# First pair's attention operands formed in place by 64-column transposes, under a new order of the work

## The chip, the cores and the metric

The kernel runs on one core of a Trainium2 chip. The metric is the device time of one execution in microseconds; below, us is microseconds and ns nanoseconds. TensorE multiplies matrices and transposes (PE, with its weight loads as PEld), VectorE is DVE, ScalarE is ACT, GpSimd is POOL, and SP issues the DMA transfers. Each engine takes its instructions strictly in the order in which they were issued to it.

## The reference

Three layers follow each other: an attention in which a query sees only keys of its own cluster (2 batches, 8 heads, 768 tokens, 64 wide, 16 centroids a head), a feed-forward layer with a soft gate and a layer norm, and a second one that multiplies two projections. All is float32.

```python
q_assign = argmax(einsum('bhsd,hcd->bhsc', q_n, c_n), -1)
k_assign = argmax(einsum('bhsd,hcd->bhsc', k_n, c_n), -1)
scores = scale * q @ k.T, where q_assign == k_assign, else -1e9
x = softmax(scores) @ v                      # to 1536 x 512
h = x @ w_in;  s = h * softmax(h)            # 512 -> 1024
x = (layernorm(s) * g_ln) @ w_out            # -> 512
out = ((x @ w_a) * (x @ w_b)) @ w_out2       # 512 -> 1536 -> 512
```

## The kernel before

Every float32 operand of a product is held as a pair hi + lo of 12-bit parts, and three of the four products are taken. Tokens sit on partitions in tiles of 128, six tiles to a head. Heads are worked in eight pairs, n = 0 to 7. One tile's step is: `score` (L727: four matmuls into a PSUM bank, the DVE maximum L731, the ACT exponential L735), `turn` (L759: six transposes, with ACT L776 and DVE L251 splitting the result into hi and lo) and, after every second tile, `apply` (L791: twelve matmuls with v, then merges L806, L811, L812 on ACT and POOL).

A head's score needs an operand block of four slots, `kqv(h)`, 128 rows by 768 tokens. Rows 0 to 63 and 64 to 127 of a slot hold different parts: q hi and q lo together, k hi twice, q hi again beside the query one-hots, k lo beside the key one-hots. Before the change that block is filled for every head in the same way. `qk_part` (L478) turns two tokens of a head at once with 128-column transposes, so that the result holds even tokens on partitions 0 to 63 and odd tokens on 64 to 127; ACT writes hi and DVE (for q, L495) or POOL (for k of the first pair, L486 and L488) writes lo into a side buffer, `hlv`. `do_place` then moves the parts to their rows: six DMAs a head (L512), save that for head 0 two of the six are ACT copies (L510, `PLACE`). For the first pair `do_sim` (L534, L535) multiplies the side buffer with the normalized centroids `cb`, DVE sums the parts (L538), `do_arg` (L591 to L602) finds the one-hot of the best centroid, and `do_oh0` (L617) turns the one-hots, which ACT (L628) and DVE (L626) write to rows 64 to 79 of two slots.

Weights arrive as the bits of float64. `weight` (L326 to L359) loads 512 of them a partition and makes float32 hi and lo: ACT or POOL scales the top word (L328, L330), DVE shifts and joins (L335, L343, L346), POOL joins the low word (L340, L350), ACT makes hi (L359) and DVE or POOL lo (L249, L251). Eight such loads make `w_in` for the first feed-forward layer, whose first matmul (L914) starts at 279 us; the four early ones are issued in the first 30 us.

The order of all this is made by a planner, `Plan`. Each work item is added with an engine, an estimated length, a rank and the buffer cells that it reads and writes. Dependencies follow the order in which the items are added; `schedule` then runs a list schedule in which each engine, when it becomes free, takes the item of lowest rank that is ready within 60 ns by the estimates, and the instructions are issued in the order found. So an estimate that is off puts an item into an engine's queue where it will wait on the chip. For a transfer the estimate is that SP is held for its cost and that it lands 1850 ns later, however many are under way:

```python
def dma(cost, rank, fn, reads, writes):
    pl.add("SP", max(cost, 650), rank, fn, reads, writes, after=1850 + min(0, cost - 650))
```

A 512 KB weight load has cost 1456 (ns); a place transfer has 275, 820 or 546 for 96, 288 or 192 KB. At the start 39 transposes of the identity (L451, `FILL`) have the lowest priority and fill TensorE's waiting time.

Of the kernel before, what the change touches and what calls it, by code (L numbers as in the profile page):

```python
# [8 lines left out]
F32 = mybir.dt.float32  # L9
# [23 lines left out]
P1 = {'a': -6.508, 's': 0.229, 'do_place': 16.159, 'do_v': -8.279, 'do_sims': 3.084, 'do_arg': -13.543, 'do_oh': -1.51, 'do_ohd': -29.092, 'qk_part': -21.079}  # L33
BR = {'h': 3.102, 'ln': 2.949, 'lnt': 7.533, 'x2': 11.917, 'dm': 0.03, 'ts': 2.583}


class Plan:
    """Work items in program order, each with its engine, an estimate of its
    length, a rank and the cells of the buffers it reads and writes. emit() issues
    them in the order of a list schedule that keeps every dependency."""  # L40
# [6 lines left out]

    def __init__(self):
        self.ops = []
        self.last = {}  # L50

    def add(self, eng, cost, rank, fn, reads=(), writes=(), after=0.0):
# [34 lines left out]
    def schedule(self):  # L87
# [9 lines left out]
        ready = {}  # L97
# [3 lines left out]
        for i in range(n):  # L101
            if not left[i]:
                ready.setdefault(ops[i][0], []).append(i)
        order = []
        while len(order) < n:
# [11 lines left out]
            end = self.pe_end(cols, s, ops[i][1]) if eng == "PE" else s + ops[i][1]  # L117
            free[eng] = end
            order.append((s, i))
            for j in succ[i]:  # L120
# [7 lines left out]
                if not left[j]:  # L128
                    ready.setdefault(ops[j][0], []).append(j)
# [8 lines left out]
def cells(buf, *spans, rows=3):  # L138
    """Cells of 128 floats of a buffer, for each half of the partitions."""
# [7 lines left out]
def dve(n):  # L147
    return n / 0.96 + 69
# [6 lines left out]
def act(n, sbuf=False):  # L155
    return n / 1.2 + (93 if sbuf else 51)

# [6 lines left out]
def tile_cluster_attention_moe_moe2(  # L164
# [1012 lines left out]
```

## Time and profile before

| | us |
|---|---|
| median of 3 runs | 747.77 |
| lowest and highest run | 745.48, 748.54 |
| span of the profiled execution | 746.8 |
| TensorE busy in it | 717.1 (96%) |
| DVE, ACT, POOL busy | 468.8, 397.9, 341.3 |
| bytes moved by DMA | 60.74 MB |

The profile of one execution lies within the three runs, 1.0 us below their median. A busy share alone says little here: it counts the fillers, and instructions that run at half clock count for twice their time. So the table is to be read by stretches, each with its idle time and its granted clock: 0 to 17.8 us until the first score, then attention with everything else beside it until 290 us, the first feed-forward layer until 450 us, and the second one, which starts at 419.5 us beside the first, to the end.

### The profile page before, as it was taken

What the parts mean: (1) busy time and instruction counts of PE and PEld (TensorE: products, weight loads), DVE (VectorE), ACT (ScalarE), POOL (GpSimd) and SP (SyncE); (2) the same over time, 40 slices, a digit from 0 to 9 for tenths busy, and PEclk for the clock granted to TensorE, in tenths of its full rate; (3) what the DMA queues carried; (4) which work ended last, traced back from release to release, by engine and by line L of the source; (5) the groups of instructions that cost most, each with busy time, mean ns of one, the idle gap of its engine ahead of it and who ended that gap; (6) DMA issues with size and microseconds to landing.
All of it is one profiled execution on the core that took longest, in us unless ns stands there. A gap on an engine that the chain in (4) does not pass through costs nothing.

```text
span 746.8 us, 12308 instructions
## 1 busy us (share of the span) xinstructions
PE 717.1 (96%) x4441; PEld 661.7 (89%) x4441; DVE 468.8 (63%) x866; ACT 397.9 (53%) x870; POOL 341.3 (46%) x429
## 2 busy tenths in 40 slices
PE   7888999999999999899899999999999999999997
PEld 7787898899999988689899999989999999999996
DVE  5995899988888887999975657631136311122222
ACT  3686898999998996565433634432133312111111
POOL 6657988958658326465513777820027300000000
PEclk7898999999999999999999999999999999999999
DMA  8774665453435001222300433320003000101011
GB/s 218 185 173 130 154 159 154 112 156 97 127 75 124 17 1 56 85 86 86 114 29 29 127 127 115 113 85 1 1 1 113 29 1 1 42 1 43 1 42 43
DMA packets 40573, 60.74 MB, mean 81 GB/s; under 512 B 3896, under 2 KB 35392, under 8 KB 40512
## 3 DMA queue, kind: packets, MB, share of 16 engines
q1 hardware_dynamic: 40512, 59.95, 28.7%
q8 instruction: 35, 0.57, 0.3%
q14 instruction: 26, 0.21, 0.1%
HBM read 36.74 MB, written 3.15 MB: 53 GB/s over the span
## 4 chain that ended last, share of the span: by engine, by line
PE 64%; DVE 16%; ACT 6%; issue 4%; POOL 4%; DMA 4%; SPq 0%; DVEq 0%; ACTq 0%; POOLq 0%
PE psS L1090 12%; PE psT L1062 11%; PE psO L791 7%; PE psS L727 6%; PE psT L759 6%; PE psM L1062 6%; PE psO L1062 6%; PE psS L914 3%; DVE F L346 3%; DVE R L251 2%; PE psO L1003 2%; POOL F L350 2%; DVE F L335 2%; PE psM L1003 2%; DMA F<-in_moe_w_b_dram 1%
## 5 line engine op out<-in xcount | busy, mean ns | idle before, releaser
L251 DVE TENSOR_TENSOR R<-psT,R 128x384 fp32r<-128x384 f32 (+1 forms) x216 | 118.1, 564 | 21.2 <-ACT R L776 19.6
L249 POOL TENSOR_TENSOR R<-F,R 128x512 fp32r<-128x512 f32 (+2 forms) x84 | 88.7, 1064 | 89.6 <-ACT R L359 80.1
L1090 PE MATMUL psS<-R 128*128 128x512 f32 x432 | 107.4, 393 | 1.4 <-ACT F L1108 1.4
L1062 PE MATMUL psT<-R 128*128 128x384 f32 x576 | 108.5, 336 | 0.0
L1062 PEld LDWEIGHTS psT<-R 128*128 128x128 f32 x576 | 102.2, 188 | 3.9
L776 ACT CAST R<-psT 128x384 fp32r<-128x384 f32 x192 | 89.9, 483 | 13.3 <-PE psT L759 11.6
L759 PE MATMUL psT<-ident,F 128*128 128x128 f32 x576 | 93.8, 279 | 3.3 <-DVE R L251 2.8
L1090 PEld LDWEIGHTS psS<-R 128*128 128x128 f32 x432 | 80.3, 188 | 16.5 <-ACT F L1108 1.8
L727 PE MATMUL psS<-R 128*128 128x512 f32 (+3 forms) x384 | 93.4, 366 | 1.0 <-ACT F L735 0.8
L731 DVE TENSOR_REDUCE mxn<-psS 128x1 f32<-128x768 f32 x96 | 91.0, 947 | 5.3 <-PE psS L727 4.4
L791 PE MATMUL psO<-R 128*128 128x256 f32 x576 | 92.6, 297 | 1.6 <-ACT F L811 0.7
L735 ACT ACTIVATE F<-psS,mxn 128x768 f32<-128x768 f32 x96 | 87.3, 909 | 3.1 <-DVE mxn L731 2.2
L791 PEld LDWEIGHTS psO<-R 128*128 128x128 f32 x576 | 75.7, 192 | 4.6 <-ACT F L811 2.7
L350 POOL TENSOR_TENSOR F<-F 128x512 int32<-128x512 int32 x45 | 60.5, 1345 | 37.4 <-DVE F L346 23.4
L727 PEld LDWEIGHTS psS<-R 128*128 128x128 f32 (+1 forms) x384 | 67.6, 195 | 11.0 <-ACT F L735 1.6
L759 PEld LDWEIGHTS psT<-ident,F 128*128 128x128 f32 x576 | 68.0, 142 | 8.5 <-DVE R L251 7.3
L1073 ACT COPY F<-psT 128x384 f32<-128x384 f32 x48 | 22.8, 478 | 97.4 <-PE psT L1062 97.4
L914 PE MATMUL psS<-R 128*128 128x512 f32 x288 | 69.2, 394 | 1.0 <-DVE F L935 1.0
L1075 ACT CAST R<-F 128x384 fp32r<-128x384 f32 x48 | 24.5, 511 | 82.5 <-DVE F L1074 82.5
L1074 DVE TENSOR_TENSOR F<-psO,F 128x384 f32<-128x384 f32 x24 | 13.3, 556 | 83.0 <-PE psO L1062 80.8
L914 PEld LDWEIGHTS psS<-R 128*128 128x128 f32 x288 | 53.0, 188 | 11.7 <-DVE F L935 1.2
L1074 DVE TENSOR_TENSOR F<-psM,F 128x384 f32<-128x384 f32 x24 | 13.3, 556 | 76.5 <-PE psM L1062 75.5
(139 smaller groups left out, 1195.3 us busy)
## 6 DMA issues: line engine op xcount, KB each, us to landing
F<-in_moe_w_out_dram SPq DMA_DIRECT2D x20, 512.0 KB, 3.3
R<-R SPq DMA_DIRECT2D x32, 288.0 KB, 5.0
R<-R SPq DMA_DIRECT2D x32, 192.0 KB, 4.9
F<-in_moe_w_a_dram SPq DMA_DIRECT2D x12, 512.0 KB, 3.4
F<-in_moe_w_b_dram SPq DMA_DIRECT2D x12, 512.0 KB, 3.4
F<-in_moe_w_in_dram SPq DMA_DIRECT2D x8, 512.0 KB, 5.4
F<-in_v_dram SPq DMA_DIRECT2D x8, 384.0 KB, 3.7
R<-R SPq DMA_DIRECT2D x30, 96.0 KB, 2.2
```

The source lines that it names most:

```text
L249: pl.add("POOL", pool(n), rank, lambda: G.tensor_tensor(out=out_, in0=in0, in1=in1, op=ALU.subtract), reads, writes)
L251: pl.add("DVE", dve(n), rank, lambda: V.tensor_tensor(out=out_, in0=in0, in1=in1, op=ALU.subtract), reads, writes)
L350: pl.add("POOL", pool(n), rank, lambda: G.tensor_tensor(out=u, in0=u, in1=low, op=ALU.add), [rk, lwk], [uk])
L727: T.matmul(sp[:, c0:c0 + cn], kq[:r, 2 * m, t * P:(t + 1) * P], kq[:r, 2 * m + 1, c0:c0 + cn], start=m == 0, stop=m == 1)
L731: pl.add("DVE", dve(S), i + SUB["max"], lambda: V.tensor_reduce(out=mxn[:, b:b + 1], in_=sp[:, :S], axis=AX.X, op=ALU.max, negate=True), [ ...
L735: pl.add("ACT", act(S) + 93 + 93, i + SUB["exp"], lambda: A.activation(F[:, po:po + 768], sp[:, :S], AF.Exp, bias=mxn[:, b:b + 1], scale=1 ...
L759: T.transpose(sp[:, c, :], pt[:, kt * P:(kt + 1) * P], ident)
L776: pl.add("ACT", act(HN), rk, lambda sp=sp, dh=dh: A.copy(dh, sp), [sk], [hk])
L791: T.matmul(psO[:, :GN], vs[:, kt, j].rearrange("p l d -> p (l d)"), pt[:, m, kt, :], start=(kt == 0 and m == 0), stop=(kt == NT - 1 and m ...
L914: T.matmul(sp[:, n0:n0 + 512], xb[:, a, c, ts_], winv[:, w, c, n0:n0 + 512], start=first, stop=(c == KD - 1 and a == 1))
L1062: T.matmul(pt[:, :BN], w[:, l, c, :], xb[:, a, c, :], start=first, stop=(c == KD - 1 and l == 1))
L1090: T.matmul(yv[t][0], hl2[a][:, ts_], wo[:, l, :], start=(first and a == 0 and l == 0), stop=(last and a == 1))
```

## The change

For both heads of the first pair `direct` takes the place of `qk_part` and `do_place`. It transposes one token parity at a time (64 columns in, 64 partitions out), twice for q and twice for k; ACT writes hi straight to its slot, one DVE instruction writes lo to its slot (for q on the other 64 partitions), and a second DVE instruction copies hi to its second slot. `do_sim0` takes the place of `do_sim` and reads these slots: for k two matmuls of 64 rows a tile, for q one of 128 rows. The DMAs and copies of `do_place` are gone for the first pair; all other pairs keep them. The planner gets a model of one DMA ring in place of a length per transfer, new lengths for matmuls (`mm_cost`) and two merges, and `ADJ`, a table of 720 numbers that are added to the ranks, by kind of work, instance and engine. The buffers, the order in which items are added outside the first pair, and the instructions of all other work are the same.

```diff
-PLACE = (0,)
-P0 = {'q': 0.676, 'a': 0.526, 's': -1.817, 'do_place': 9.179, 'do_v': -4.684, 'do_sim': 1.842, 'do_arg': 0.4, 'do_oh0': 7.789}
+P0 = {'q': 0.676, 'a': 0.526, 's': -1.817, 'do_v': -4.684, 'do_sim0': 1.842, 'do_arg': 0.4, 'do_oh0': 7.789}
+ADJ = {
+    "apply0 0 PE": -1.431, "apply0 1 PE": 65.455, "apply0 2 PE": 54.006, "apply0 3 PE": -288.832,
...
+    "load_win ACT": 306.443, "load_win DVE": 250.077, "load_win POOL": 765.326, "load_win SP": 46.393,
...
+}
...
-        self.ops.append((eng, cost, rank, fn, deps, after))
+        keys = (f"{self.tag[0]} {eng}", f"{self.tag[0]} {self.tag[1]} {eng}") if self.tag else ()
+        self.keys.append(keys)
+        self.ops.append((eng, cost, rank + sum(ADJ.get(x, 0.0) for x in keys), fn, deps, after))
+    ISSUE, HEAD, TAIL, SLOW, DEPTH = 560.0, 950.0, 900.0, 1.6, 7000.0
...
-            end = self.pe_end(cols, s, ops[i][1]) if eng == "PE" else s + ops[i][1]
-            free[eng] = end
+            if eng == "PE":
+                end = free[eng] = self.pe_end(cols, s, ops[i][1])
+            elif eng == "SP":
+                ring = max(ring, s + self.HEAD) + ops[i][1] * self.SLOW
+                free[eng] = max(s + self.ISSUE, ring - self.DEPTH)
+                end = ring + self.TAIL
+            else:
+                end = free[eng] = s + ops[i][1]
...
+def mm_cost(n, k):
+    return (n / 2.4 + 14.5) * k
...
-        pl.add("SP", max(cost, 650), rank, fn, reads, writes, after=1850 + min(0, cost - 650))
+        pl.add("SP", cost, rank, fn, reads, writes)
...
+    def direct(n, x, hf, r, rk, bk):
+        i = 1 if x else 0
+        pt = bank[bk][:D, :HN]
+        kq, ko = kqv(2 * n + hf), kqo(2 * n + hf)
+        cs = slice(r * HN, (r + 1) * HN)
+        lo, hi = slice(0, D), slice(D, P)
...
+        def tr():
+            for a in range(HT):
+                T.transpose(pt[:, a * P:(a + 1) * P], nat[i][:, hf, 2 * a + r], ident)
+
+        pl.add("PE", 330, rk, tr, [natk(i, (hf,)), "ident"], [bk])
+        s0, s1, s2, sc, r1, r2 = (1, 1, 3, 1.0, hi, lo) if x else (0, 2, 0, scale, lo, hi)
+        k1, k2 = (2, 1) if x else (1, 2)
+        h = kq[lo, s0, cs]
+        pl.add("ACT", act(HN), rk, lambda: A.activation(h, pt, AF.Copy, scale=sc), [bk], [key(s0, 1)])
+        pl.add("DVE", dve(HN), rk, lambda: V.scalar_tensor_tensor(
+            out=kq[r2, s2, cs], in0=pt, scalar=sc, in1=h.bitcast(F32),
+            op0=ALU.mult, op1=ALU.subtract), [bk, key(s0, 1)], [key(s2, k2)])
+        pl.add("DVE", dve2(HN), rk + 0.5, lambda: V.tensor_copy(kq[r1, s1, cs], h.bitcast(F32)), [key(s0, 1)], [key(s1, k1)])
+
+    def do_sim0(n, s, f, rk, bk):
...
+            for t in range(NT):
+                ts_ = slice(t * P, (t + 1) * P)
+                if s:
+                    T.matmul(pv[:, t], kq[:D, 1, ts_], cw[:D, :, 0], start=True, stop=False)
+                    T.matmul(pv[:, t, 0], kq[:D, 3, ts_], cw[:D, 0, 0], start=False, stop=True)
+                else:
+                    T.matmul(pv[:, t], kq[:, 0, ts_], cb[:, o:o + 64], start=True, stop=True)
...
-            if n == j == 0 and part in PLACE:
-                pl.add("ACT", act((d1 - d0) * HN, True), rk, lambda dst=dst, src=src: A.copy(dst, src.bitcast(F32)), rd, wr)
-            else:
-                dma(cost, rk, lambda dst=dst, src=src: Y.dma_start(dst.bitcast(F32), src.bitcast(F32)), rd, wr)
+            dma(cost, rk, lambda dst=dst, src=src: Y.dma_start(dst.bitcast(F32), src.bitcast(F32)), rd, wr)
...
-                    at(f, e, qk_part, x, f, tail=("psM" if f else f"psT{x}",))
-                    at(f, e + 1, do_sim, x, f, tail=("psM" if f else f"psS{x}",))
+                    for r in range(2):
+                        at(f, e + 0.3 * r, direct, x, f, r, tail=("psM" if f else f"psT{r}" if x else f"psS{r}",))
+                    at(f, e + 1, do_sim0, x, f, tail=("psM",))
...
-                for part in range(3):
-                    at(f, 2.5 + P0["q"] + part * 0.2, do_place, f, part)
...
-        pl.add("PE", 665, i + SUB["qk"], mm, [rc((ko + t * P, P), (ko + 768, 768), (ko + 1536 + t * P, P), (ko + 2304, 768))], [sk])
+        pl.add("PE", mm_cost(512, 2) + mm_cost(256, 2), i + SUB["qk"], mm, [rc((ko + t * P, P), (ko + 768, 768), (ko + 1536 + t * P, P), (ko + 2304, 768))], [sk], after=70.0)
...
-            pl.add("ACT", act(GN), rk, lambda: A.copy(xv[hi], psO[lo, :GN]), ["psO"], [hk])
+            pl.add("ACT", act(GN) + 110, rk, lambda: A.copy(xv[hi], psO[lo, :GN]), ["psO"], [hk])
```

## Rows read from the trace of the kernel before

**Rows 1.** The page's head: the span.
```profile
span 746.8 us, 12308 instructions
```

**Rows 2.** Busy time by stretch: length, five engines (instructions), granted clock, DMA share, GB/s.
```profile
0.00:17.80 17.80, 13.44 (x70) 12.59 (x71) 8.85 (x29) 6.62 (x13) 11.49 (x38) 0.75 0.80 218
17.80:40.00 22.20, 18.86 (x102) 15.54 (x101) 20.28 (x36) 15.43 (x35) 13.38 (x14) 0.82 0.67 180
...
50.00:70.00 20.00, 16.20 (x94) 13.75 (x95) 12.67 (x26) 12.98 (x30) 12.00 (x14) 0.84 0.54 139
...
100.00:280.00 180.00, 176.83 (x1314) 163.80 (x1314) 160.87 (x290) 168.05 (x407) 120.89 (x180) 1.00 0.40 102
...
300.00:320.00 20.00, 17.37 (x88) 14.12 (x87) 19.97 (x43) 12.72 (x21) 9.29 (x11) 1.00 0.22 75
...
360.00:380.00 20.00, 17.54 (x103) 15.81 (x102) 18.04 (x38) 8.41 (x19) 9.10 (x9) 0.91 0.33 107
...
420.00:487.00 67.00, 64.79 (x400) 61.63 (x399) 41.33 (x57) 30.29 (x59) 49.62 (x45) 1.00 0.37 118
487.00:741.60 254.60, 254.40 (x1336) 238.06 (x1337) 65.94 (x107) 55.42 (x109) 28.24 (x24) 1.00 0.08 27
```

**Rows 3.** Chain that ended last, first 40 us: start, length, what.
```profile
3.54 8.86 DMA F<-in_moe_w_in_dram
```

**Rows 4.** Timeline of the first 18 us: start, length, engine, line, work [idle before <-releaser].
```profile
3.70 1.28 ACT L485 ACT_TABLE_LOAD   x1 [3.70 <-DMA F<-in_k_dram]
...
5.49 0.49 ACT L491 ACTIVATE R<-psT 128x384 fp32r<-128x384 f32 x1
...
6.01 0.56 DVE L495 SCALAR_TENSOR_TENSOR R<-psT,R 128x384 fp32r<-128x384 f32 x1 [0.77 <-ACT R L491]
...
7.10 0.59 DVE L459 TENSOR_TENSOR cb<-psM,cb 64x128 fp32r<-64x128 f32 x2 [0.53 <-ACT cb L458]
...
7.84 0.27 PE L534 MATMUL psS<-cb,R 128*128 128x64 f32 x1 [1.25 <-DVE cb L459]
...
8.69 0.36 DVE L538 TENSOR_REDUCE F<-psS 128x96 f32<-128x192 f32 x1 [0.99 <-PE psS L535]
...
9.08 0.25 DVE L591 TENSOR_REDUCE mx<-F 128x6 f32<-128x96 f32 x1
...
9.27 0.37 PE L535 MATMUL psS<-cb,R 128*128 128x32 f32 x1
...
11.63 0.21 DVE L602 TENSOR_SCALAR F<-F 128x96 f32<-128x96 f32 x1
...
13.11 0.43 DVE L335 TENSOR_SCALAR F<-F 128x512 int32<-128x512 int32 x1 [1.11 <-ACT F L328]
...
15.40 0.84 PE L617 MATMUL psT<-ident,F 128*64 128x128 f32 x3
...
17.37 1.46 DVE L335 TENSOR_SCALAR F<-F 128x512 int32<-128x512 int32 x1
...
17.82 1.51 PE L727 MATMUL psS<-R 128*128 128x512 f32 x4
```

**Rows 5.** Timeline of the first 7 us: fillers (L451) and k's and q's transposes (L478).
```profile
1.35 2.82 PE L451 MATMUL psO<-ident 128*128 128x128 f32 x12 [1.35 <-POOL half L418]
...
3.96 1.49 PE L478 MATMUL psT<-ident,F 128*128 128x128 f32 x6
...
5.66 0.93 PE L451 MATMUL psO<-ident 128*128 128x128 f32 x7
```

**Rows 6.** Timeline from 44 to 60 us, SP's queue and POOL.
```profile
44.36 5.75 SPq L512 DMA_DIRECT2D R<-R  x6
...
50.21 0.54 SPq L326 DMA_DIRECT2D F<-in_moe_w_in_dram  x1
...
58.06 1.60 POOL L330 TENSOR_SCALAR F<-F 128x512 f32<-128x512 f32 x1 [6.56 <-DMA F<-in_moe_w_in_dram]
```

**Rows 7.** Who TensorE waited for, whole span: us in total, times, longest.
```profile
PE psO L1003 <- DVE R L251: 2.5, 1, 2.5
```

More of the change, by code (lines that the diff above doesn't have):

```diff
@@ L46 @@
     BOOT = 600.0
+    ENGINES = ("PE", "DVE", "ACT", "POOL", "SP", "NOP")
     def __init__(self):
@@ L50, in __init__ @@
         self.last = {}
+        self.tag = None
+        self.keys = []
     def add(self, eng, cost, rank, fn, reads=(), writes=(), after=0.0):
@@ L96, in schedule @@
         free = {}
-        ready = {}
+        ring = 0.0
+        ready = {e: [] for e in self.ENGINES}
         start = [0.0] * n
@@ L102, in schedule @@
             if not left[i]:
-                ready.setdefault(ops[i][0], []).append(i)
+                ready[ops[i][0]].append(i)
         order = []
@@ L128, in schedule @@
                 if not left[j]:
-                    ready.setdefault(ops[j][0], []).append(j)
+                    ready[ops[j][0]].append(j)
         self.start = start
@@ L292, in task, with tag_of @@
         tasks.append((rank, len(tasks), fn, args))
+    def tag_of(name, args):
+        if name in ("score", "turn", "apply"):
+            return name + (f"{args[1]}" if name == "apply" else ""), args[0] // 12
+        if name in ("moe2_ab", "moe2_y"):
+            return name, 0
+        if name in ("load_w2", "moe_x2"):
+            return name, f"{args[0]}.{args[1]}"
+        if name in ("qk_part", "direct", "do_sims", "do_sim0", "do_place", "do_v", "do_oh", "do_ohd", "do_load", "do_oh0", "do_arg"):
+            return name, f"{args[0]}.{args[1]}" if name != "do_arg" else f"{args[0]}.{args[1][0]}.{args[2][0]}"
+        return name, args[0] if args else 0
     def run_tasks():
         for _, _, fn, args in sorted(tasks, key=lambda x: x[:2]):
+            pl.tag = tag_of(fn.__name__, args)
             fn(*args)
+        pl.tag = None
         tasks.clear()
@@ new lines, in do_sim0, with mm @@
+    def do_sim0(n, s, f, rk, bk):
+        hp = pairs[n][1]
+        kq, ko = kqv(2 * n + f), kqo(2 * n + f)
+        o = hp * 192 + f * 128
+        cw = cb[:, o:o + 64].rearrange("p (l r c) -> p l r c", l=2, r=2)
+        ng = 2 if s else 4
+        pv = bank[bk][:, :NT * ng * C].rearrange("p (t g c) -> p t g c", t=NT, g=ng)
+        def mm():
+            for t in range(NT):
[5 more added lines that the diff above has]
+                    T.matmul(pv[:, t], kq[:, 0, ts_], cb[:, o:o + 64], start=True, stop=True)
+        rd = [rc((ko + 768, 768), (ko + 2304, 768), rows=1)] if s else [rc((ko, 768))]
+        pl.add("PE", NT * 109 * (2 if s else 1), rk, mm, [*rd, "cb"], [bk])
+        pl.add("DVE", dve(NT * ng * C), rk, lambda: V.tensor_reduce(
+            out=sim[:, :, f, s].rearrange("p a r c -> p r a c"),
+            in_=pv.rearrange("p (r a) g c -> p r a c g", r=2), axis=AX.X, op=ALU.add), [bk], [part("sim", (s,), (f,))])
@@ L521, in do_v @@
             out=vl, in0=src, in1=vh.bitcast(F32), op=ALU.subtract), [natk(2)], [ck])
-    def do_sim(n, s, f, rk, bk):
-        hp = pairs[n][1]
-        hl = hlv(n)
-        sh, sl = ((2, 0), (1, 3))[s]
-        o = hp * 192 + f * 128
-        pv = bank[bk][:, :HT * 64].rearrange("p (a l x) -> p a l x", a=HT, l=2)
-        def mm():
-            for a in range(HT):
-                ts_ = slice(f * HN + a * P, f * HN + (a + 1) * P)
-                T.matmul(pv[:, a], hl[:, sh, ts_], cb[:, o:o + 64], start=True, stop=False)
-                T.matmul(pv[:, a, 0], hl[:, sl, ts_], cb[:, o:o + 32], start=False, stop=True)
-        pl.add("PE", HT * 218, rk, mm, [hlk(n, [sh, sl], 1 << f), "cb"], [bk])
-        pl.add("DVE", dve(HT * 64), rk, lambda: V.tensor_reduce(
-            out=sim[:, :, f, s].rearrange("p a r c -> p a (r c)"),
-            in_=pv.rearrange("p a l x -> p a x l"), axis=AX.X, op=ALU.add), [bk], [part("sim", (s,), (f,))])
     def do_sims(n, s, rk, bk):
@@ L795, in apply @@
             rd += [(vso(n) + kt * 256 + j * P, P) for kt in range(part * HT, (part + 1) * HT)]
-            pl.add("PE", 6 * 109, i + SUB["pv"] + 1 + part, mm, [rc(*rd)], ["psO"])
+            pl.add("PE", mm_cost(GN, 6), i + SUB["pv"] + 1 + part, mm, [rc(*rd)], ["psO"], after=70.0)
             return
@@ L810, in apply @@
                 tk = fc((to, 256), rows=1 << j)
-                pl.add("ACT", act(GN), rk, lambda: A.copy(tv[hi], psO[hi, :GN]), ["psO"], [tk])
+                pl.add("ACT", act(GN) + 110, rk, lambda: A.copy(tv[hi], psO[hi, :GN]), ["psO"], [tk])
                 pl.add("POOL", pool(GN), rk, lambda: G.tensor_tensor(
```

93 lines of the change are left out of this document (87 added, 6 removed), and 113 rows, old and new, of the table ADJ.

## The prediction

> **What bounds the kernel now.** The span is 746.8 us [rows 1]. TensorE's busy share of it says little, as it counts half-clock time and filler, so the view to start from is the busy time by stretch [rows 2]. For each stretch I take as loss the idle time of TensorE plus its busy time times what the granted clock lacks of 1.00. From 487 to 741.6 us the loss is 0.2 us: the second feed-forward layer runs at TensorE's pace, and nothing in the change shortens it. From 100 to 280 us it is 3.2, from 420 to 487 it is 2.2. The losses worth a look are 0 to 17.8 us (no score before that, so nearly the whole stretch), 17.8 to 40 (3.3 idle + 0.18 x 18.86 = 6.7), 50 to 70 (3.8 + 0.16 x 16.2 = 6.4), 300 to 320 (2.6) and 360 to 380 (2.5 + 0.09 x 17.54 = 4.0). So TensorE bounds the kernel nearly everywhere, and at a few places something holds it up. What that is, I read in the chain, the timeline and the list of waits.
>
> At the start the chain runs for 8.86 us through a load of `w_in` [rows 3], which has nothing to do with the first score: ACT's scaling of that load (L328) stands in ACT's queue, and DVE's shift behind it (L335) makes DVE wait 1.11 us ahead of the last of the first head's one-hots [rows 4]. From 17.8 to 40 us DVE is the bound: busy 20.28 of 22.2 us, TensorE waiting at part clock [rows 2]. Near 58 us POOL has stood still for 6.56 us for one more load of `w_in`, which SP issued at 50.21 behind six place transfers and which landed 7.8 us later [rows 6]. By the old plan it lands 1456 + 1850 ns = 3.3 us after its issue, so the plan set an instruction into POOL's queue 4.5 us too early, and what TensorE needed from POOL stood behind it. In 300 to 320 us DVE is busy 19.97 of 20 [rows 2], a true bound. In 360 to 380 us it is one wait of 2.5 us for DVE's L251 [rows 7].
>
> **The change, part by part.** *Way to the first score.* Only head 0 counts here. ACT loads its table until 4.98 [rows 4]. The four groups of three transposes take 12 x 0.25 us (six L478 took 1.49) from 3.96 [rows 5], so until 6.95; the last ACT write of hi (0.49, as L491) ends at 7.44, the last DVE lo (0.56, as L495) at 8.0, and the centroid parts, if they come last (L459, 0.59), at 8.6. Then 12 matmuls for k: the 12 of before took 1.80 us (7.84 to 9.64), so 10.4. The sum (L538, 0.36) gives 10.8, the six one-hot steps of 0.21 to 0.28 (L591 to L602) 1.5 us more, 12.3. For q the sum reads twice as much (0.36 + 0.2, 192 more elements at about the pace of L538) and five steps take 1.25: 14.1. Three transposes of the one-hots (L617) take 0.84, two writes behind them 0.98: 15.9, with handoffs 16.0 against 17.82 [rows 4]. Gain 1.8 us. The 1.11 us of waiting is gone here, and so are the two shifts for `w_in`, which ranks can set later. The four copies of hi on DVE lie in the 1.8 us in which the sums wait for the matmuls. No row shows such a copy; the nearest is L335, one source and one target in SBUF, 0.43 us alone and 1.46 us where it ran beside POOL's L350 [rows 4]. I take 0.43, as POOL loses the k split in this stretch, and four of them fit the gap. At 1.46 they take 5.8, of which 4.0 stick out and make the gain a loss of 2.2; if the one-hots of k hide behind q's work the gain is 4.
>
> *Transposes and the clock.* Twelve more transposes and twelve more matmuls for the pair are 12 x 0.25 [rows 5] + 12 x 0.15 (1.80 / 12 [rows 4]) = 4.8 us. What of them is not on the path above stands where TensorE ran fillers or waited, and costs 0; without that cover head 1's half costs 2.4. At the start twelve fillers took 2.82 us, 0.24 each; seven of them at 5.66 took 0.93, 0.13 each, with nothing but transposes before [rows 5]: TensorE went from its lower level to the upper. The Trainium skill (TensorE: Matmul & The Clock Gate, Part 4: PE-mode transpose) says that transposes do not engage the full clock. By it the twelve matmuls behind the new transposes would run at the lower level, up to 1.8 us more, an estimate; the row contradicts it, and the row decides.
>
> *Head 1 and DVE, 17.8 to 40 us.* Per head DVE gains three lo writes (3 x 0.56), four copies (4 x 0.43) and 0.2 for the longer sum: 3.6 us [rows 4] for head 1, where DVE is the bound. Against it, ranks can move a shift for `w_in` of 1.46 us and its like out of it, POOL loses the k split, so that less runs beside DVE, and six transfers (1152 KB) leave the ring. I take 0, with ends of 7.7 lost (3.6, and four copies at 1.46 instead of 0.43) and 3.4 gained (half of the stretch's loss).
>
> *The plan for transfers, 50 to 70 us.* For the load issued at 50.21 [rows 6] the new plan adds the transfers ahead of it at 1.6 times their cost: six places are 2 x (275 + 820 + 546) x 1.6 = 5.3 us from 45.3 on, then 2.3 for the load and 0.9, about 54.4. That is 0.9 us later than the old plan had it, more if the ring was not empty at 44.36, yet still ahead of 58. What helps more is the rank: `w_in`'s work on POOL goes back by 765 (one load's by 86), so POOL takes whatever of attention is ready first, and nothing needs `w_in` before 279 us. Gain 5.5 of 6.4; ends 0 and 6.4.
>
> *Ranks elsewhere.* 360 to 380: the single wait and the part clock beside it go together, 4.0, ends -2 and 6.6 (with 300 to 320, which I leave as DVE's bound). 100 to 280: 2.0 of 3.2, ends -4 and 3.2. 420 to 487: 1.0 of 2.2, ends -2 and 2.2 [rows 2]. From 487 on: 0. The new lengths of matmuls and merges only feed the plan.
>
> *Sum.* 1.8 + 0 + 5.5 + 4.0 + 2.0 + 1.0 = 14.3; 746.8 - 14.3 = 732.5 us for a profiled execution. The median of the runs stands 1.0 above the profiled span, so 733.5.
>
> **The rivals.** *DVE takes over in the first 40 us.* The copies meet POOL: head 0 loses 2.2 instead of gaining 1.8, head 1 costs 7.7. With 12.5 gained elsewhere: 746.8 + 2.2 + 7.7 - 12.5 + 1.0 = 745.2, within the noise. For it: L335 at 1.46 against 0.43 us [rows 4]. Against it: POOL's own work there falls. The Trainium skill (SBUF — State Buffer, SBUF: two separate sides) has a rule for it, which speaks against a copy on DVE: DVE and GpSimd share a port pair, and whichever starts first holds it for its whole instruction. The trace agrees, with 1.46 us beside POOL's L350.
>
> *The new order does little outside the pair.* Only the 1.8 us stay: 746.0. For it: the list schedule takes what is ready, so ranks matter only where several items are. Against it: the stall at 58 us is just such a place.
>
> *Slower: a new wait at the head of a queue.* Ranks now move by hundreds, against one a tile in the attention. If a POOL instruction is set ahead of its load as L330 is now, the price is that of today's stall, 6.4 us a time [rows 2, 6]. Place: POOL between 20 and 110 us, where the late `w_in` loads are split. Two such waits take back 12.8 of the 14.3; the third decides for slower: 732.5 + 19.2 + 1.0 = 752.7. Against it: the ring model and the late rank both work to prevent this.
>
> *All losses go.* 4 + 3.4 + 6.4 + 6.6 + 3.2 + 2.2 = 25.8: 746.8 - 25.8 + 1.0 = 722.0.
>
> **How the numbers follow.** The forecast has 58% (726 to 743 us), all losses gone 18%, no change by either of the two rivals 12%, the slower one 12%. 0.5%, about what a measurement of this kernel can tell from no change, is 3.7 us. Faster by more: 0.58 + 0.18 = 0.76; within: 0.12; slower by more: 0.12. The range reaches from just under the case in which all goes, 720, to the upper runs of no change, 749, and leaves out most of the slower case and a little at the lower end.
>
> **What would show it.** Right: the first score near 16 us; no POOL wait of several us for `w_in` before 110 us; the granted clock at 1.00 in 50 to 70 and 360 to 380; the last layer's length as now. Wrong: copies of hi near 1.46 us, DVE full in the first 40 us and the second head's scores later; a new single wait of several us in any queue; or a first score as early as said while the end comes no earlier, which would mean that the time is given back in DVE's stretch.

## The result

| | before | after |
|---|---|---|
| median, us | 746.89 | 754.12 |
| lowest to highest run | 745.48 to 748.54 | 752.84 to 757.73 |
| ratio, 95% interval | | 1.0106 (1.0075 to 1.0137) |
| span of the profiled execution | 746.8 | 751.0 |

The change makes the kernel slower by 7 to 8 us. 733.5 was forecast, and the time lies above the range. Below, "A against B" is the difference of their two ratios to the kernel before, with the half-widths of both intervals added in squares; 0.1% is 0.75 us. The profiled execution of after took 752.84 us with a span of 751.0: 1.84 us lie around the span.

The first rows of the kernel after, of the view of busy time by stretch, are to be read against [rows 2] (length; PE, PEld, DVE, ACT, POOL busy with instructions; granted clock; DMA share; GB/s):

```profile
span 751.0 us, 12433 instructions
```

```profile
0.00:17.80 17.80, 13.07 (x88) 11.14 (x89) 13.38 (x38) 7.45 (x15) 9.46 (x35) 1.00 0.47 150
17.80:40.00 22.20, 17.48 (x94) 15.19 (x93) 18.75 (x39) 12.77 (x29) 8.03 (x9) 0.77 0.30 101
50.00:70.00 20.00, 17.49 (x127) 15.45 (x125) 15.31 (x30) 15.74 (x38) 13.59 (x18) 1.00 0.71 180
80.00:100.00 20.00, 16.08 (x109) 14.82 (x108) 18.47 (x28) 15.83 (x38) 14.78 (x23) 0.92 0.53 135
100.00:280.00 180.00, 177.67 (x1324) 164.77 (x1323) 158.41 (x287) 167.78 (x406) 122.30 (x180) 1.00 0.41 101
300.00:320.00 20.00, 16.46 (x80) 13.22 (x78) 19.31 (x38) 9.04 (x16) 10.67 (x11) 1.00 0.21 72
320.00:360.00 40.00, 37.68 (x207) 31.94 (x208) 39.41 (x80) 22.73 (x36) 23.75 (x24) 0.96 0.27 91
360.00:380.00 20.00, 18.03 (x126) 16.43 (x125) 19.05 (x46) 9.95 (x22) 10.69 (x11) 1.00 0.34 107
420.00:487.00 67.00, 66.73 (x435) 64.36 (x434) 33.74 (x51) 23.83 (x50) 34.96 (x30) 1.00 0.24 79
```

Two stretches of the kernel before that the prediction did not need, the same view:

```profile
80.00:100.00 20.00, 19.02 (x142) 17.81 (x143) 17.44 (x33) 18.85 (x47) 17.68 (x26) 1.00 0.52 119
320.00:360.00 40.00, 39.03 (x251) 35.23 (x250) 39.29 (x86) 22.21 (x39) 23.96 (x24) 1.00 0.28 93
```

With the prediction's own measure of loss (TensorE's idle time, plus its busy time times what the clock lacks of 1.00):

| stretch, us | loss before | loss after | change | forecast |
|---|---|---|---|---|
| to the first score | 17.8 | 16.8 | -1.0 | -1.8 |
| 17.8 to 40 | 6.7 | 8.7 | +2.0 | 0 |
| 50 to 70 | 6.4 | 2.5 | -3.9 | -5.5 |
| 80 to 100 | 1.0 | 5.2 | +4.2 | 0 |
| 100 to 280 | 3.2 | 2.3 | -0.9 | -2.0 |
| 300 to 360 | 3.6 | 7.4 | +3.8 | 0 |
| 360 to 380 | 4.0 | 2.0 | -2.0 | -4.0 |
| 420 to 487 | 2.2 | 0.3 | -1.9 | -1.0 |

Every stretch in which a gain was forecast shows one, 9.7 us together. Three others give 10.0 back. The spans differ by 4.2 us; the 4 that the table lacks lie in TensorE's added work (2.4 by the prediction's price for the second head) and in the stretches left out, and are not told apart. Two rows hold less than they seem, as the section on the reasons shows: the first, and 360 to 380, where the gain is work that now waits in the row above it.

The largest new loss is one instruction. Timeline of the kernel after at 91 us (start, length, engine, line, work; in brackets the idle time before it and what ended it):

```profile
90.29 1.97 POOL L718 TENSOR_TENSOR R<-F,R 128x384 fp32r<-128x384 f32 x2
...
91.48 3.23 DVE L1076 TENSOR_SCALAR rinv<-rsum 128x4 f32<-128x4 f32 x1 [0.25 <-ACT F L991]
...
92.24 0.50 POOL L472 TENSOR_SCALAR R<-F 128x384 fp32r<-128x384 f32 x1
...
92.71 1.29 POOL L580 TENSOR_TENSOR F<-F 128x512 int32<-128x512 int32 x1
...
93.97 0.71 POOL L1068 TENSOR_TENSOR F<-F 64x256 f32<-64x256 f32 x1
94.65 0.98 POOL L796 TENSOR_TENSOR R<-F,R 128x384 fp32r<-128x384 f32 x1
94.74 0.18 DVE L1078 RECIPROCAL rinv<-rinv 128x4 f32<-128x4 f32 x1
...
95.68 1.01 DVE L467 TENSOR_TENSOR R<-psT,R 128x384 fp32r<-128x384 f32 x2
...
96.28 0.55 PE L1015 MATMUL psT<-ident,F 128*128 128x128 f32 x3 [2.58 <-DVE R L467]
```

DVE adds 1e-9 to four numbers a partition, which takes 0.15 us at the least and 0.22 in the median of the 24 times that it is done. Here it starts 0.78 us ahead of the end of a POOL instruction (the second L718) and ends with the third one after that (94.71 and 94.68). DVE counts as busy throughout, so no wait of DVE is listed; only TensorE's 2.58 us, far behind it in DVE's queue, points there.

### The profile page after: what moved, and what is told of

Same layout as the page of the kernel before. It is cut to its first block, busy times and chain, and to the rows that moved or that the text cites. A ratio compares the mean times of both kernels' runs of the same rounds, so it can differ in the third digit from the quotient of the medians.

```text
span 751.0 us, 12433 instructions
## 1 busy us (share of the span) xinstructions
PE 718.3 (96%) x4465; PEld 660.5 (88%) x4465; DVE 476.2 (63%) x880; ACT 398.9 (53%) x872; POOL 339.4 (45%) x425
## 4 chain that ended last, share of the span: by engine, by line
PE 72%; DVE 16%; ACT 5%; issue 3%; POOL 3%; DMA 0%; DVEq 0%; POOLq 0%; ACTq 0%
PE psT L1318 13%; PE psS L1346 13%; PE psO L1318 7%; PE psM L1318 7%; PE psO L1047 7%; PE psT L1015 6%; PE psS L983 6%; PE psS L1170 3%; DVE R L467 2%; PE psM L1259 2%; PE psO L1259 2%; DVE F L576 2%; ACT F L991 1%; DVE F L565 1%; DVE bst L1193 1%
## 5 line engine op out<-in xcount | busy, mean ns | idle before, releaser
L465 POOL TENSOR_TENSOR R<-F,R 128x512 fp32r<-128x512 f32 (+2 forms) x84 | 90.5, 1084 | 96.0 <-ACT R L589 71.1
L1346 PE MATMUL psS<-R 128*128 128x512 f32 x432 | 107.2, 393 | 0.0
L1015 PE MATMUL psT<-ident,F 128*128 128x128 f32 x576 | 92.0, 279 | 8.1 <-DVE R L467 5.6
L580 POOL TENSOR_TENSOR F<-F 128x512 int32<-128x512 int32 x45 | 61.5, 1366 | 41.9 <-DVE F L576 32.1
L1170 PE MATMUL psS<-R 128*128 128x512 f32 x288 | 71.2, 401 | 3.4 <-DVE F L1191 3.4
L1332 DVE TENSOR_TENSOR R<-F,R 128x384 fp32r<-128x384 f32 x48 | 30.8, 641 | 67.2 <-ACT R L1331 67.2
L1318 PE MATMUL psO<-R 128*128 128x384 f32 x288 | 53.8, 334 | 0.0
```

What stands on the lines that cost most here:

```text
L465: pl.add("POOL", pool(n), rank, lambda: G.tensor_tensor(out=out_, in0=in0, in1=in1, op=ALU.subtract), reads, writes)
L580: pl.add("POOL", pool(n), rank, lambda: G.tensor_tensor(out=u, in0=u, in1=low, op=ALU.add), [rk, lwk], [uk])
L1015: T.transpose(sp[:, c, :], pt[:, kt * P:(kt + 1) * P], ident)
L1170: T.matmul(sp[:, n0:n0 + 512], xb[:, a, c, ts_], winv[:, w, c, n0:n0 + 512], start=first, stop=(c == KD - 1 and a == 1))
L1318: T.matmul(pt[:, :BN], w[:, l, c, :], xb[:, a, c, :], start=first, stop=(c == KD - 1 and l == 1))
L1346: T.matmul(yv[t][0], hl2[a][:, ts_], wo[:, l, :], start=(first and a == 0 and l == 0), stop=(last and a == 1))
```

## The experiments

**Each part alone, planned anew.** e1 is the kernel after with `ADJ = {}`. e2 is the kernel before with `direct` and `do_sim0` for the first pair under its old plan. e3 is the kernel before with the new ring model and lengths, and e4 adds the table of ranks to e3.

> The changed kernel with its rank table empty: new forming of the first pair's operands, new plan for transfers and matmul lengths, old ranks. If the rank table is what loses time, this is at 747 us or below (ratio to the kernel before 1.00 or less, against 1.0106 of the change). If the forming of the operands loses (DVE has 3.6 us more a head), it stays near 754. If the ranks gain and something else loses more, it is above 754.

> The kernel before with the new forming of the first pair's operands alone; plan, lengths and ranks as before. If DVE's added work in the first 40 us is the loss: about 751 to 754 us. If the order of the work is the loss: 744 to 747, the first score near 16.8 us as in the changed kernel, the stall of POOL near 58 us still there.

> The kernel before with the new plan for transfers and the new lengths of matmuls and merges, old operands, no rank table. If the ring model does what was forecast, the POOL stall near 58 us shrinks and the time falls to about 741 to 744 us. If the new model misplaces other work, it is at 750 or above.

> The kernel before with the new plan and the rank table (which leaves out the old forming of the first pair's operands), old operands. If the order is the loss, it is about as slow as the changed kernel, 751 to 756 us. If the operands are the loss, 747 or below. As the ranks were set for other operands, a time above 756 would tell that the order is fragile, not which part of it.

| | median, us | ratio | 95% |
|---|---|---|---|
| e1 | 763.18 | 1.0231 | 1.0187 to 1.0275 |
| e2 | 766.14 | 1.0256 | 1.0217 to 1.0295 |
| e3 | 757.93 | 1.0148 | 1.0114 to 1.0183 |
| e4 | 764.09 | 1.0232 | 1.0199 to 1.0264 |

All four are slower than before, three of them slower than the whole change; e2 lies 12 us above the higher of its two theories. The ranks are worth 9 us with the new operands (e1 against after) and cost 6 with the old ones (e4 against e3). So a part planned anew does not measure the part: whatever alters the plan alters the whole order. From here on each kernel's order is written out as a list of places, and only what is named moves.

**The forming, under either order.** f1 keeps the order of before and forms the first pair's operands anew. f2 keeps the order of after and forms them in the old way.

```diff
-            i = min((c for c in ready[eng] if est[c] <= t + self.WINDOW), key=lambda c: (ops[c][2], c))
+            _, i = heapq.heappop(heap)      # ready items by their PLACES
```

> The kernel before with its order written out as a list of places, so that nothing is planned anew, and only the first pair's operands formed as in the kernel after; each new instruction stands where the one it replaces stood. It is compared with the kernel before. Theory A, the forming itself costs: head 1's four groups go one after the other through the one bank psM and put off its first score, about 3 us as in the kernel after; first score about 1 us earlier, second head's first score 2 to 4 us later, end 1 to 4 us later. Theory B, the forming gains or is neutral and the new order alone costs: the end no later than before, 1 us earlier to 1 us later. Were the 20 us of e2 due to the forming, the end would be over 10 us later.

> The kernel after with its order written out as a list of places, and only the first pair's operands formed as in the kernel before (with its transfers), each at the place of the new ones. It is compared with the kernel after, whose median is about 754. Theory A, the forming costs about 3 us: 749 to 752. Theory B, the order costs and the forming is neutral: 753 to 756, so again 6 to 10 us above the kernel before. If the new order relies on the shorter way, some us above 754.

f1: 748.75 us, 1.0041 (1.0017 to 1.0066). f2: 753.50 us, 1.0094 (1.0063 to 1.0126), 0.1% under after, within 0.44%. The forming costs 3 us under the old order, theory A of f1. Under the new one the old forming brings nothing back, theory B of f2: what after loses lies in its order and in how the new instructions stand in it. In f2's profile the addition to the row sums is held as well (3.24 us at 93.70), so that wait comes with the order and not with the new operands.

**The held DVE instruction.** f3 is the kernel after with the addition replaced; the row sums are at least 1, so that 1e-9 changes nothing in float32.

```diff
-        pl.add("DVE", 72, i + 1, lambda: V.tensor_scalar(
-            out=rinv, in0=rsum[:, n % 2, g], scalar1=1e-9, scalar2=None, op0=ALU.add), [rm], ["rinv"])
+        pl.add("DVE", 72, i + 1, lambda: V.tensor_reduce(
+            out=rinv, in_=rsum[:, n % 2, g].unsqueeze(3), axis=AX.X, op=ALU.max), [rm], ["rinv"])
```

> The kernel after with the same order on every engine; only the 24 DVE instructions that add 1e-9 to the row sums ahead of the reciprocal are replaced by a reduction over an axis of length one (the addition of 1e-9 is left out). In the kernel after the one at 91.5 us took 3.23 us where others take 0.15, beside POOL's five instructions in a row. Theory A, that is a wait for something that DVE and POOL share, which a reduction does not need: it takes 0.1 to 0.3 us there, and the end comes 2 to 3.5 us earlier, about 751. Theory B, DVE is held by something else, or TensorE waits for another engine then anyway: within 1 us of the kernel after.

750.48 us, 1.0057 (1.0038 to 1.0075), against after 0.49% less, within 0.36%: theory A, 3.7 us. The instruction's durations in the kernel after and in f3 (ns: shortest/median/longest):

```profile
L1076 DVE TENSOR_SCALAR rinv<-rsum x24: 153/224/3232, 46.7 to 284.7; 128x4 f32<-128x4 f32 x24
```

```profile
L1076 DVE TENSOR_REDUCE rinv<-rsum x24: 135/147/159, 49.2 to 281.9; 128x4 f32<-128x4 f32 x24
```

In f3 it runs in 0.16 us in the midst of the same POOL instructions. g3 makes the same edit in the kernel before:

> The kernel before, its order unchanged on every engine; only the 24 DVE instructions that add 1e-9 to the row sums are replaced by a reduction over an axis of length one (the addition of 1e-9 is left out), as f3 does with the kernel after. Longest of them before: 0.84 us, and 0.155 in the median. If the 3.2 us that f3 took away belong to the new order, this changes the kernel before by less than 1 us. If the instruction costs in any order, it gains 2 us or more.

746.28 us, 0.9999 (0.9978 to 1.0019). The old order never put the two together for long (its longest took 0.84 us), so the loss belongs to the new order and not to the instruction as such.

**The second head: bank or DVE.** In the kernel after all four groups of the second head pass through the bank `psM`, and its first score comes 23.26 us behind the first head's (40.04 - 16.78; before 37.24 - 17.82 = 19.42). g1 is f3 with the groups of odd tokens in `psO` and with what follows of that head 2.5 us earlier in the list, g2 is f3 with the second head's copies on ACT:

```diff
-tail=("psM" if f else f"psT{r}" if x else f"psS{r}",)
+tail=(("psM", "psO")[r] if f else f"psT{r}" if x else f"psS{r}",)        # g1
-        pl.add("DVE", dve2(HN), rk + 0.5, lambda: V.tensor_copy(kq[r1, s1, cs], h.bitcast(F32)), ...
+        pl.add("ACT", act(HN, True), rk + 0.5, lambda: A.copy(kq[r1, s1, cs], h.bitcast(F32)), ...   # g2, where hf is 1
```

> The kernel f3 with its order written out; of the second head's four groups the two of odd tokens go through the bank psO instead of psM, each directly behind its partner of even tokens, and what follows of that head (its sums, one-hots and their turn) stands 2.5 us earlier in the list. It is compared with f3, about 750.5. Theory A, the single bank psM holds back the second head: TensorE no longer waits for DVE's lo writes ahead of the transposes (0.7 and 1.3 us), the second head's first score comes 1.5 to 3 us earlier against the first head's, end 748 to 749.5. Theory B, DVE is full until then and the bank changes nothing: the second head's first score within 0.8 us of f3 against the first head's, end 750 to 751.

> The kernel f3 with its order written out; only the second head's four copies of hi go from DVE to ACT, at the same places. Compared with f3, about 750.5. Theory A, DVE is what is late in the first 40 us: its four copies (0.35 to 1.3 us each, 2 to 4 us in all) leave it, the second head's first score comes 1 to 3 us earlier and the end 748 to 750. Theory B, the second head waits for the bank or for ACT: no change, or up to 1 us later as ACT's copies stand ahead of its hi writes.

g1: 750.59 us, 1.0053 (1.0036 to 1.0071), the same as f3 within 0.25%. Its sums' matmuls start at 23.3 us, in f3 at 28.3, and yet the second head's first score comes at 42.22 against 42.61. Against the first head's, as the expectation counts it, that is 22.42 against 23.93 us: 1.5 us earlier, the low end of theory A. The end is that of theory B, so the bank may cost the second head something, but it does not set the time. g2: 749.07 us, 1.0034 (1.0016 to 1.0051), 0.23% under f3, within 0.25%: in theory A's direction, too small to be told from nothing by itself.

**All copies on ACT.** h1 is f1, h3 is f3 and i2 is the kernel after, each with the eight copies of hi on ACT, the first head's behind its four hi writes.

> The kernel f1 (the order of before, the first pair's operands formed anew, 3 us slower than before) with all eight copies of hi on ACT instead of DVE, those of the first head behind its four hi writes. Theory A, the forming costs because DVE carries the copies in its fullest stretch: the first score comes 1 to 2 us earlier than in f1 under the same clock, the median 745.5 to 747, no slower than before. Theory B, the longer way (four hi and lo writes one after another, one bank) costs: within 1 us of f1, 748 to 750.

> The kernel g2 (the kernel after with the sums by a reduction and the second head's copies on ACT) with the first head's four copies on ACT too, behind its four hi writes. Theory A, the copies on DVE hold back the first head's sums (k's sums start 0.85 us after its matmuls end in the kernel after): first score 0.5 to 1 us earlier, end 747.5 to 749. Theory B, the first head waits for its one-hots and their turn anyway: no change, 749 to 750.

> The kernel after with its order written out and only the eight copies of hi on ACT; the sums stay as they are, with the addition that was held for 3.23 us at 91.5 us. Theory A, the copies cost 3 to 4 us by themselves, as between f3 and h3: 749.5 to 751. Theory B, with the first two heads earlier the DVE instruction no longer meets POOL's five instructions, and both losses go at once: 746 to 748, as h3.

| | median, us | ratio | 95% | against |
|---|---|---|---|---|
| h1 | 747.70 | 1.0009 | 0.9985 to 1.0033 | f1: -0.32%, within 0.34% |
| i2 | 750.40 | 1.0061 | 1.0037 to 1.0085 | after: -0.45%, within 0.39% |
| h3 | 746.64 | 0.9987 | 0.9963 to 1.0011 | after: -1.19%, within 0.39%; f3: -0.70%, within 0.30% |

Theory A in i2 and h3. h1 leans to it, no slower than before, but its 0.32% under f1 are within the noise and its median lies above theory A's 747. i2 takes the copies away alone (the addition still takes 3.23 us there, and TensorE is busy for 16.79 of the 20 us from 80 on) and gains 3.4 us; with f3's edit as well the kernel after is no slower than before. The copies, in the kernel after and in i2 (ns), and the first scores of both heads in each:

```profile
L752 DVE CAST R<-R x8: 353/510/1351, 6.0 to 25.5; 64x384 fp32r<-64x384 f32 x8
```

```profile
L852 ACT CAST R<-R x8: 504/508/518, 7.6 to 23.5; 64x384 fp32r<-64x384 f32 x8
```

```profile
16.78 1.66 PE L983 MATMUL psS<-R 128*128 128x512 f32 x8
...
40.04 0.95 PE L983 MATMUL psS<-R 128*128 128x512 f32 x4
```

```profile
16.23 1.65 PE L1083 MATMUL psS<-R 128*128 128x512 f32 x8
...
35.11 0.94 PE L1083 MATMUL psS<-R 128*128 128x512 f32 x4
```

On ACT each takes 0.51 us wherever it stands. On DVE the second head's four take 3.34 us (timeline: 0.55, 1.80 for two, 0.99), and its first score comes 4.9 us later than with them on ACT. The long ones seem held by POOL, as the addition is: the one of 1.35 us starts at 22.51 while POOL's L580 runs until 23.65, the one of 0.99 at 25.54 while POOL's L465 runs until 26.32, and both end 0.21 us after that instruction. Of the eight, the two with no POOL instruction beside them took 0.35.

**The stall at 58 us.** The new order takes it away, and so do the next kernels under the old order. f4 is the kernel before with the instructions on POOL, DVE and ACT that split two loads of `w_in` 5 and 6 us later in the list; h2 puts the start of the second load's splitting 16 us later instead of 5, and its end 6.

> The kernel before with its order written out, TensorE's unchanged, and only the instructions on POOL, DVE and ACT that split two loads of w_in moved some places back, so that the one for which POOL stood still for 6.56 us near 58 us comes behind work for the attention. Theory A, the prediction's term of 5.5 us for that stall is right and is lost again elsewhere in the kernel after: the end 4 to 6.5 us earlier than before, 741 to 743. Theory B, the stall hides another wait (DVE, or the transfers of the places): 0 to 3 us earlier. Theory C, the work that is put back gets in the way later: no change or later.

> The kernel f4 (the order of before with the splitting of one load of w_in put behind the attention's work near 58 us), and the splitting of the next load put back too, behind the attention's merges of 72 to 80 us, where f4 gave its gain back. Theory A, the gain of f4 was lost to that one load: the 3.5 us that f4 gave back in 70 to 80 us stay, end 742 to 745. Theory B, POOL has so much attention work up to 140 us that whatever is put back is late again: 746 to 749, and the time is lost at another place before 140 us.

f4: 748.28 us, 1.0029 (1.0010 to 1.0047), no gain. h2: 743.62 us, 0.9964 (0.9939 to 0.9990), faster than both kernels; 0.65% under f4, within 0.31%. Busy time by stretch of f4, its waits from 70 to 84 us (engine, what it writes, line, who released it; us in total, times, longest), and the same two stretches of h2:

```profile
50.00:70.00 20.00, 18.93 (x137) 16.77 (x136) 16.06 (x32) 17.16 (x41) 13.16 (x16) 1.00 0.57 143
70.00:80.00 10.00, 6.99 (x45) 5.78 (x44) 8.20 (x16) 5.58 (x15) 8.34 (x11) 0.92 1.07 255
```

```profile
ACT F L913 <- POOL R L356: 3.3, 1, 3.3
...
PE psT L866 <- DVE R L358: 2.4, 2, 1.8
POOL F L437 <- DMA F<-in_moe_w_in_dram: 1.5, 1, 1.5
```

```profile
50.00:70.00 20.00, 18.71 (x137) 16.78 (x136) 16.06 (x32) 17.16 (x41) 13.18 (x16) 1.00 0.54 141
70.00:80.00 10.00, 9.21 (x72) 8.59 (x71) 9.75 (x19) 8.62 (x21) 9.77 (x17) 1.00 1.06 217
```

In f4 the stall is gone (TensorE 18.93 of 20 us busy, before 16.20), theory C all the same: 14 us later the next load's splitting, set ahead of the attention's merges, takes its place. POOL waits 1.5 us for that load, ACT 3.3 for POOL, TensorE 1.8 at a time for DVE behind them. With that load behind the attention's work too the gain stays: theory A of h2. In its profile the seventeenth of the 96 scores starts at 67.97, before at 74.31, and the last at 271.95 instead of 277.15.

g4 puts five other weight loads, three of `w_in` and two of `w_out`, 90 us later in the list, transfers and splitting alike.

> The kernel before with its order written out; five weight loads (the last four of w_in that are split between 50 and 110 us, and two of w_out behind them, so that buffers follow each other as before) stand 90 us later, transfers and splitting alike, where POOL is busy for 54 of 100 us. Theory A, the loss between 50 and 140 us is POOL's and DVE's work for the weights beside the attention: that stretch loses 5 to 8 us less than before, 1 to 3 of them come back as losses between 140 and 280, end 740 to 744. Theory B, what sets 50 to 140 us is the attention's own DVE, ACT and place transfers: no change, 745 to 749. Theory C, the work lands where TensorE has no slack either (98.7 of 100 us busy): later than before.

751.49 us, 1.0067 (1.0043 to 1.0090): theory C. The load that POOL stands still for at 58 us was not among the five (POOL stands still for 7.05 us there in g4), so it tells nothing of that stall. From 140 to 280 us TensorE is busy for 133.0 of 140 us, before 138.2: POOL's idle time there is not free.

**Both together.** i1 has the places of h2 and the operands of h1.

> The order of before with both edits that helped it: the first pair's operands formed as in h1 (eight copies on ACT) and the two loads of w_in split later as in h2. If the two add, it is as fast as h2, 2 to 5 us under before (743 to 745), since h1 alone was no faster than before. If the stretch without transfers of places lets the loads of w_in land earlier as well, 1 us more; if the forming takes time that the stall at 58 us had hidden, 745 to 747.

747.00 us, 1.0011 (0.9987 to 1.0035), 0.47% above h2, within 0.35%. The new forming, without copies on DVE, costs nothing under the order of before (h1) and about 3.5 us under that of h2. In i1's profile 1.3 us of it are there at the first score and 2.2 at the second head's; why is not settled.

## Why the prediction was wrong

**What failed** is three steps. The first is the term "four of them fit the gap" and "I take 0" for the copies on DVE: 3.4 us (i2 against after). The second is a loss that no step had, the DVE instruction held beside POOL: 3.7 us (f3). Both together are 8.9 us (h3 against after), as much as the 7 to 8 by which after is slower. What is left of the change is then worth 0 and not 14.3, and the third step says where a part of that went: the 4.0 of "ranks elsewhere" with 300 to 320 left "as DVE's bound". From 300 to 380 us the new order loses 2 to 3 us more than the old one, and in h3 too.

The division into the first two is not the only one. In f2 there are no copies, and the new order with the old operands is still 0.94% slower than before, 7.0 us, of which the held addition is 3.7 by f3's measure, an estimate. The 3.4 us of the copies are thus what the new operands could have gained in that order and did not; i2 lies 0.33% under f2, within 0.40%, so that this gain itself is not clear of the noise.

**Way to the first score, 1.8.** The total was right, partly by luck, and the base was wrong. 16.0 us were worked out; without the copies on DVE it is 16.23 (i2) and 16.12 (h3). But in i2 k's matmuls end at 8.97 and not at 10.4 (ACT loads its table at 0.72 us and not until 4.98, and the matmuls are faster), and the last of the one-hots ends at 14.72 and not at 14.1: beside POOL single steps take up to 0.95 us, where 0.21 to 0.28 were taken from rows that in the trace of before have steps of 0.55, 0.73 and 1.05 among them. The 17.82 of before hold a stretch at TensorE's lower clock that the next execution need not have. Busy time from 8 to 16 us of before and of f4, whose instructions are the same up to then:

```profile
8.00:12.00 4.00, 3.88 (x22) 3.48 (x21) 3.23 (x12) 0.00 (x0) 1.95 (x3) 0.60 1.03 258
12.00:16.00 4.00, 2.36 (x11) 2.24 (x12) 2.00 (x3) 2.20 (x4) 3.14 (x4) 0.50 0.76 164
```

```profile
8.00:12.00 4.00, 3.54 (x30) 3.06 (x29) 3.28 (x8) 1.72 (x3) 3.62 (x5) 1.00 1.06 295
12.00:16.00 4.00, 1.69 (x12) 1.22 (x12) 3.94 (x10) 1.75 (x5) 2.99 (x4) 1.00 1.08 224
```

f4's first score starts at 16.45. The clock is not all that differs: the first load of `w_in`, issued at 3.54 in both, lets ACT's scaling start at 12.42 in before and at 9.40 in f4, so the 1.11 us that the prediction counts as DVE's wait for it may be a part of the 1.4. After and f3, where that scaling starts at 9.78 and 9.96, are the better pair: 16.78 at 1.00, 18.68 at 0.66 and 0.50, and 0.56 of these 1.90 us are there already when k's sums start (9.79 and 10.35). Like with like, 16.45 against 16.78 and 17.82 against 18.68, the change makes the first score 0.3 to 0.9 us later, and 0.2 to 0.3 earlier with the copies on ACT; each of these is a single execution. The copies' place was misjudged: they were to lie while the sums wait for the matmuls, but q's lo writes stand in that gap too. DVE of the kernel after:

```profile
7.79 1.01 DVE L749 SCALAR_TENSOR_TENSOR R<-psS,R 64x384 fp32r<-64x384 f32 x2
8.81 1.05 DVE L752 CAST R<-R 64x384 fp32r<-64x384 f32 x2
9.79 0.34 DVE L774 TENSOR_REDUCE F<-psM 128x96 f32<-128x192 f32 x1
```

The last of k's twelve matmuls starts at 8.75 and takes 0.25; the sums start at 9.79, 0.8 us later. The size was right (0.35 alone, 0.53 here), the gap was full. The 0.43 us that the prediction takes for L335 "alone" were not quite that: POOL's L520 started 0.09 us behind it, so DVE was first.

**Transposes and the clock.** Right: the twelve matmuls take 0.11 us apart, at the upper level, behind nothing but transposes and fillers. The price of 0.15 had the slow ones of before in it.

**Second head and DVE, 0 with ends of -7.7 and 3.4.** The bound was right, the value was not. The copies took 0.45 to 1.35 us and not 0.43, 3.34 together. What was set against them, the shifts for `w_in` that ranks can move out, hardly left: on DVE they take 3.8 us from 17.8 to 40, before 4.7, and two of them are still among this head's writes (timeline: L565 at 16.38, 1.39 us, and L576 at 18.38). Of the rival "DVE takes over in the first 40 us" the mechanism, copies that meet POOL, is right, and 2.0 us of loss, or 3.8 by the distance of the two first scores, are what came of its 7.7; it was wrong in the 12.5 us that it left standing elsewhere.

**Stall at 58 us, 5.5.** Right in place, and in size half of it to nearly all: 3.9 us less loss in after, 2.7 us by the ratio of h2 (0.7 to 4.6), 5.2 at the last score of its profile. The terms given for the landing add up to 53.8 and not 54.4, which needs the load's own issue at 50.21; either lies ahead of 58. The rule behind it was incomplete. POOL's 6.56 us were counted as free once the load came later, but the load's splitting on POOL, 5.1 us in the timeline of before (1.60 in [rows 6], and 0.89, 1.30 and 1.27 behind it), has to stand somewhere, and up to 140 us POOL is nearly full: in f4 the next load took it all back.

**360 to 380 (4.0), 100 to 280 (2.0), 420 to 487 (1.0).** The last two came out at 0.9 and 1.9. The first did not: its 2.0 is offset by 300 to 360, "left as DVE's bound" and so counted at 0, which loses 3.8 more. Taken as one stretch, 300 to 380 loses 7.5 us before and 9.3 after; in the other profiles it is 6.2 to 8.0 under the old order (f1, f4, g3, g4, h1, h2, i1) and 9.2 to 11.6 under the new one (f2, f3, g1, g2, h3, i2). The view of busy time, before and after:

```profile
300.00:380.00 80.00, 73.94 (x439) 65.15 (x438) 77.30 (x165) 43.34 (x78) 42.36 (x43) 0.98 0.28 92
```

```profile
300.00:380.00 80.00, 72.17 (x411) 61.58 (x410) 77.76 (x161) 41.72 (x73) 45.11 (x45) 0.98 0.27 90
```

DVE is full in both. That a bound can become worse was not asked. What makes it worse can be read in the weights' shifts on DVE from 300 to 380, after and before (busy us, mean ns):

```profile
L576 DVE SCALAR_TENSOR_TENSOR F<-F 128x512 int32<-128x512 int32 x13 | 11.0, 842 | 0.0
L565 DVE TENSOR_SCALAR F<-F 128x512 int32<-128x512 int32 x13 | 6.6, 504 | 0.0
```

```profile
L346 DVE SCALAR_TENSOR_TENSOR F<-F 128x512 int32<-128x512 int32 x13 | 9.3, 714 | 0.0
L335 DVE TENSOR_SCALAR F<-F 128x512 int32<-128x512 int32 x13 | 5.5, 431 | 0.0
```

The same 26 instructions take 2.8 us more. Nearly all of it lies in four of them, which start while a POOL instruction for the weights runs, as here at 332 us:

```profile
332.58 1.41 POOL L580 TENSOR_TENSOR F<-F 128x512 int32<-128x512 int32 x1 [3.13 <-DVE stt L1197]
...
332.86 1.68 DVE L576 SCALAR_TENSOR_TENSOR F<-F 128x512 int32<-128x512 int32 x1
```

They take 1.68, 1.72, 0.92 and 1.07 us, and 0.69 or 0.41 without such a meeting; before, two meet one (1.02 and 0.67). So the loss at 91 us and this one look the same in the traces: DVE behind POOL, counted as busy. No run here took these four away, so their worth is read and not measured.

**The slower rival, 12%.** Its direction is right, its mechanism is not, and that its 752.7 lies near 754.1 is luck: no POOL instruction stands ahead of a load of `w_in` for long in the kernel after. POOL does stand still once for 13.45 us, until 39.77, for ACT's L715 (its longest wait there before was 5.17), but in h3, as fast as before, it does so for 10.6. The wait that costs sits on DVE, counts as busy time, and in the trace of before the same line never took more than 0.84 us.

**Base.** "The median stands 1.0 above the span" was one of three runs. 1.84 us lie around the span here, so the profiled execution of before took about 748.6, an estimate, 1.7 above its median of 746.9, and not below it as the section on the time before has it; that of after was 1.3 below its own. This hid 3 us of the loss in the two profiles: 4.2 by the spans, 7.2 by the medians.

## What to carry to other kernels

Price an instruction that is added to the fullest engine by what stands in the gap that is to hide it, not by its own length, and ask first whether an idle engine can take it: the same eight copies cost about 3 us on DVE and nothing that shows on ACT. Look for DVE instructions that start while POOL runs: the wait is counted as busy time, and only the spread of one line's durations shows it. A gain from a removed stall counts only when the work that caused it has a named new place with room; otherwise it is the next load's stall. Where a list schedule makes the order, write the order out before a part is tried by itself, and compare the first microseconds of two profiles at the same granted clock.

## What the runs showed of the hardware

A DVE addition of 128x4 float32 numbers from SBUF to SBUF took 3.23, 3.23 and 3.24 us in three kernels (after, i2, f2), at the same place beside the same POOL instructions, and a reduction of the same numbers 0.16 us beside them (f3, h3). The Trainium skill (SBUF — State Buffer, SBUF: two separate sides) says that DVE and GpSimd share a port pair and that, of a GpSimd instruction and a DVE instruction that takes the pair, whichever starts first has it for its whole instruction. The trace agrees for the two long copies of the second head, which end 0.21 us after the POOL instruction that they met. If the addition got in once the POOL instruction that was running had ended, it would have waited 0.78 us; the trace has it wait for three more, back to back, and end as the third of them does, although POOL goes on with a fourth (L796 at 94.65). The measurement decides: here the wait was longer than one instruction. Why DVE got in there and not earlier, and what the two engines contended for, no run shows directly.

The clock at the start is not the same from one execution to the next: the same instructions had 0.60 and 0.50 in one and 1.00 in another from 8 to 16 us (before and f4), and 0.66 and 0.50 in f3 where after had 1.00, which is worth about 1.3 us at the first score (18.68 and 16.78, less the 0.56 by which k's sums started later), an estimate. From 4 to 8 us TensorE had been busy for 2.75 us in before and 3.42 in f4, but f3, with 3.09, lost the clock and after, with 2.92, kept it, so the cause stays open.
